# Attention, gated feed-forward and routed experts in one launch: load costs of the instruction planner, the low part of the weights, and softmax sums from a column of ones

## The chip, the cores and the metric

One core of one Trainium2 chip runs the kernel in a single launch. The metric is the device time of that launch in microseconds (us). The kernel before was run three times: 729.37, 726.54 and 720.55 us, median 726.54 us. One more execution was profiled; it took 723.54 us.

## The reference

Three layers follow each other.

- **Attention with hash buckets.** For 2 batches x 8 heads, 768 queries and 768 keys of 64 numbers. Six random projections give each query and key a bucket of 6 sign bits; a query sees only keys of its own bucket. `scores = q @ k.T / 8`, -1e9 where the buckets differ, then softmax over the keys and `attn @ v`. The softmax divides by `sum(exp) + 1e-9`.
- **A dense layer with a rational activation** on the 1536 x 512 result: `h = x @ w_in` (512 x 2048), `g = P(h) / Q(h)` with a cubic P and a quadratic Q, then `g @ w_out` (2048 x 512).
- **Routed experts.** Each of the 1536 rows goes to the expert of 8 with the largest logit: `relu(x @ w1[e]) @ w2[e]` (512 x 1024 x 512), scaled by its softmax weight and by a sigmoid gate.

All is float32. The kernel keeps the precision by splitting each operand into a high and a low float16 part, and sums three products (high x high, low x high, high x low).

## The kernel before, in words

**Stages.** 12 tiles of 128 rows. For each tile 8 heads are attended (96 in all), and each tile then passes the dense layer in 4 units (48 in all). The two run interleaved: the units of a tile begin some tiles behind its heads. When all tiles are through, the rows are ranked by expert, gathered in slots of 128 and sent through the experts (the last stage, from `early` and `final` to `tail`).

**A head** (`attend`, L518): TensorE makes the scores in PSUM (`scb`), VectorE takes their maximum (L533) and two small numbers (L534, L535), ScalarE takes the exponential into `p` and with `accum_out` its row sum into `den` (L540). A split (`split`, L284) makes a float16 high part on ScalarE or VectorE (L287) and a low part on GpSimd or VectorE (L288), both in `phl`. A transposing DMA turns them into `pT` (L544), and 18 matmuls with the split values VH and VL (L549 to L551) give 64 columns of PV in PSUM bank 0. The first `n32` = 7 heads go another way (`pv32`): transposed in float32 by TensorE, copied out of PSUM (L509), multiplied in float32 (L513). After each 4 heads `finish` (L553) forms the divisors `dn` from `den` (L561, L562), multiplies PV by them into `xf` (L563) and splits the result.

**The weights of the dense layer** come as 32 chunks of 512 KB (L402) in four buffers `tmp`. Each chunk holds its float32 numbers as halves of int64 words with scaled exponents; VectorE builds them with three integer instructions (L403, L404, L405). ScalarE then writes the high part WH, scaled by 256 (L406), scales the float32 chunk itself by 256 in place (L408), and GpSimd or VectorE subtracts (`WL = tmp - WH`, L409).

**What sets the order.** The program is written as a graph of operations, each with an engine (some with a choice of two), a cost, a DMA cost and a priority. `Graph.order` lays them out in time by these costs: it takes the operation that can start first, among those the one of the lowest priority number, and assigns a free operation to the engine that would end it first. Every engine's instructions then stand in the order of their planned starts, and each engine works them off strictly in that order on the chip. So a cost that is off does not change what is computed, but where an instruction stands: behind one that has to wait, it waits too. A load of 512 KB stands there with 1.456 us of the DMA queues. The table TUNE adds an offset to the priorities of each kind of operation (by its tag and by one of four parts of the program) and a bias to the choice of engine.

Of the kernel before, what the change touches and what calls it, by code (L numbers as in the profile page):

```python
# [25 lines left out]
TUNE = dict(lo=(0, 0, 1), w0=-6, n1=24, nb=[3, 3, 4, 4], nt=4, n2=4, q1=(1, 0), ck=[0, 1], ck2=[0, 0], cq=1, cq2=0, wq=1, wp=[1], wd=1.0, pq=3, pk=2, ld=5, lag=2.5, wdma=1.0, win=0.02, c0=0, cv=[2, 4], cv1=(0, 2), tc=4, ka=(0, 0, 0, 1), kb=(0, 0, 0, 0), wx=(0,), n32=7, vp=2, ev=(0, 0), c2=(1, 1, 1, 1), v2=(0, 0, 0, 0), fu=120, ff=14, fm=0.1, off={'cp': (-268.29, 167.43, -111.57, 0), 'ev': -227.13, 'ex': (660.02, 1353.36, 1191.8, 1674.11), 'f1': (-424.84, 428.14, -10.04, 621.04), 'f2': (-250.37, -7.79, -220.05, -301.11), 'f3': (-23.35, 4.25, 226.88, 33.9), 'f4': (-1229.72, -691.2, -403.07, -1036.86), 'f5': (208.7, 465.9, -29.69, 201.32), 'f7': (96.16, -302.05, -323.07, 73.51), 'f8': (-949.66, -1170.66, -563.08, -423.14), 'f9': (1185.88, 741.58, 588.87, 694.19), 'fa': (-813.71, -671.7, -732.04, -973.72), 'fb': (-76.95, -16.38, 5.69, 102.6), 'fi': (-682.61, -1081.59, -735.33, -615.52), 'gh': (-188.08, -241.89, -88.65, -81.64), 'gl': (475.63, 349.79, 802.09, 243.69), 'h': (-620.4, -273.02, -317.42, -644.08), 'hi': (749.27, 786.31, 760.64, 1215.18), 'k0h': 800.69, 'k0l': 127.42, 'kd': (-36.59, -32.48, 0, 0), 'kh': -286.24, 'kl': 26.57, 'lo': (471.66, -228.06, 668.92, 516.9), 'm2': (606.86, 1243.54, 1044.04, 1707.71), 'mx': (865.18, 876.13, 337.17, 72.6), 'pj': (332.41, -110.01, 246.4, 0), 'pv': (-157.74, -18.43, -210.46, -244.93), 'qh': (-522.1, -565.46, -401.0, 0), 'ql': (1130.36, 1000.63, 1003.49, 0), 'sc': (-674.28, -1622.43, -1312.02, -720.34), 'sg': (-1186.42, -501.8, -575.81, 0), 'tp': (-366.12, -394.82, 100.39, -477.05), 'tr': -356.17, 'v0h': 53.58, 'v0l': 122.21, 'v3': -200.82, 'vd': (103.76, 43.76, 0, 0), 'vh': -341.41, 'vl': -180.9, 'w1': 199.23, 'w2': 612.34, 'w3': 83.55, 'wd': -102.43, 'wh': 26.96, 'wl': 316.54, 'ws': 21.9, 'xd': (-547.65, 103.84, -621.18, -153.75), 'xh': (371.61, 427.76, 443.42, -215.44), 'xl': (-523.69, -754.73, -621.28, -525.38), 'xt': (-403.22, -1195.83, -1445.94, -248.18), 'xx': (159.21, -73.33, 571.84, -141.72), 'xy': (1693.3, 791.35, 722.59, 1567.91), 'xz': (443.87, -71.3, -641.46, -59.94)}, bias={'cp': (-7.42, 'ACT', 'ACT', 0), 'ev': 18.62, 'f3': (44.43, 25.58, 25.55, 39.82), 'gh': (0.32, 32.1, None, 22.27), 'gl': (30.91, 28.24, 3.36, 8.31), 'hi': (37.76, 60.01, 45.16, 50.31), 'k0h': -7.13, 'k0l': -29.55, 'kh': 'DVE', 'kl': -16.62, 'lo': (23.46, 27.97, 61.28, 7.14), 'qh': (7.28, -13.66, 25.19, 0), 'ql': (3.88, 12.77, 2.89, 0), 'v0h': 16.3, 'v0l': 17.12, 'vh': -3.05, 'vl': 13.82, 'wh': 11.09, 'wl': 0.49, 'ws': None, 'xh': None, 'xl': (0.16, 0.79, 'DVE', 2.33), 'xx': ('DVE', 'DVE', 'DVE', None)}, rel={('v', 0, 0): 28.6, ('v', 0, 1): 33.0, ('w', 3): 10.6, ('w', 1): 3.3, ('w', 4): 11.7, ('w', 2): 9.3, ('v', 0, 2): 0, ('v', 0, 3): 6.8})  # L26


class Graph:
# [19 lines left out]
    def op(self, eng, cost, fn, r=(), w=(), dma=0.0, prio=None, deps=(), tag=None, alt=(), rel=0.0):  # L49
# [243 lines left out]
def kernel_body(ctx, tc, qt_, kt_, v, proj, wio, ab, wg, w1, w2, cst, out):  # L293
# [811 lines left out]
```

## Time and profile before

| | before |
|---|---|
| median of 3 runs | 726.54 us (720.55 to 729.37) |
| profiled execution | 723.54 us |
| its span, first to last instruction | 721.8 us |
| mean granted TensorE clock | 0.969 |
| VectorE busy / ScalarE busy / GpSimd busy | 584.6 / 544.1 / 311.7 us |
| TensorE matmuls busy | 622.3 us |
| DMA, mean over the span | 165 GB/s |

How to read it: a busy time is a sum over stages with different limits. The last stage takes the span from about 522 us on. Matmuls are pipelined, each is recorded longer than the engine is held by it, so a busy TensorE is not one at its limit. In groups of instructions a line can be that of a helper (`split` has L287 and L288 for many tiles), so groups go by line and by tiles. The engines are named PE (TensorE), PEld (its weight loads), DVE (VectorE), ACT (ScalarE), POOL (GpSimd) and SP (the queue that issues the DMAs).

### The profile page before, as it was taken

The numbers are of one execution on the slowest core, as the hardware profiler recorded it, in microseconds if no ns is written. First come the engines' busy times: TensorE is split into PE (matmuls) and PEld (weight loads), VectorE is DVE, ScalarE is ACT, GpSimd is POOL, SyncE is SP. The second block draws the span as 40 slices with busy tenths as digits, with TensorE's granted clock in tenths as the row PEclk, the third lists the DMA queues.
The fourth block names the chain that finished last, engine by engine and source line by source line (L and its number), as shares of the span: only waits on it lengthen the run. The fifth ranks groups of instructions, "written<-read, shape, count | busy, mean of one in ns | idle before, by whom it ended". The sixth has DMA issues, their size and how long they took to land. (4 is left out here: it accounts for less than half of the span.)

```text
span 721.8 us, 19612 instructions
## 1 busy us (share of the span) xinstructions
PE 622.3 (86%) x7721; PEld 451.1 (62%) x7721; DVE 584.6 (81%) x1132; ACT 544.1 (75%) x885; POOL 311.7 (43%) x229
## 2 busy tenths in 40 slices
PE   0288699699998998989998999999689899989994
PEld 0146567567676765757776757777357577667762
DVE  5898778899998999795989996898949666576664
ACT  6587668889988888988996999987625565565663
POOL 2002326566656656476654574635403322122231
PEclk9999899799999999999999999999989999999997
DMA  8798639876969988979686496951753677799852
GB/s 273 232 221 275 177 93 209 173 117 120 169 104 174 190 150 182 173 137 183 127 158 132 83 164 122 169 91 24 208 144 88 126 205 248 251 243 264 230 132 40
DMA packets 230390, 119.04 MB, mean 165 GB/s; under 512 B 208398, under 2 KB 213390, under 8 KB 230288
## 3 DMA queue, kind: packets, MB, share of 16 engines
q1 hardware_dynamic: 227088, 111.37, 71.9%
q0 software_dynamic: 3200, 6.30, 2.6%
q8 instruction: 66, 1.08, 0.6%
q14 instruction: 36, 0.29, 0.1%
HBM read 83.15 MB, written 7.34 MB: 125 GB/s over the span
## 5 line engine op out<-in xcount | busy, mean ns | idle before, releaser
L288 POOL TENSOR_TENSOR phl<-p,phl 128x768 f16<-128x768 f32 x89 | 150.1, 1692 | 92.0 <-ACT phl L287 56.2
L598 PE MATMUL bank<-XT,WH 128*128 128x128 f16 x1440 | 130.4, 222 | 8.6 <-DVE tmp L620 5.4
L598 PEld LDWEIGHTS <-WH 128*128 128x128 f16 x1536 | 121.9, 99 | 20.5 <-issue 9.3
L932 DVE SCALAR_TENSOR_TENSOR WL<-st,WH 128x1024 f16<-128x1024 f32 x88 | 102.8, 1218 | 36.3 <-ACT WH L929 36.1
L598 PE MATMUL bank<-XT,WL 128*128 128x128 f16 x720 | 126.6, 221 | 0.0
L625 PE MATMUL bank<-WH,G 128*128 128x512 f16 x352 | 104.7, 379 | 4.8 <-DVE X L633 4.8
L540 ACT ACTIVATE p<-scb,sm 128x768 f32<-128x768 f32 x96 | 94.9, 990 | 14.1 <-DVE sm L535 6.9
L533 DVE TENSOR_REDUCE sm<-scb 128x1 f32<-128x768 f32 x96 | 90.4, 949 | 18.0 <-PE scb L527 12.9
L929 ACT ACTIVATE WH<-st 128x1024 f16<-128x1024 f32 x88 | 87.4, 1048 | 18.1 <-DMA st<-in_w 17.4
L625 PEld LDWEIGHTS <-G 128*128 128x128 f16 x576 | 52.2, 98 | 64.5 <-ACT G L287 3.5
L946 PEld LDWEIGHTS <-WH 128*128 128x128 f16 x1024 | 80.2, 99 | 9.9 <-issue 7.2
L288 POOL TENSOR_TENSOR G<-tmp,G 128x512 f16<-128x512 f32 x48 | 59.1, 1235 | 47.9 <-ACT G L287 44.9
L961 PE MATMUL bank<-WH,HT 128*128 128x512 f16 x256 | 76.7, 379 | 3.0 <-DVE HT L954 1.5
L969 POOL DMA_INDIRECT out<-OS,idx x16 | 21.8, 1361 | 131.5 <-ACT OS L965 101.2
L598 PEld LDWEIGHTS <-WL 128*128 128x128 f16 x768 | 76.1, 99 | 0.0
L287 ACT ACTIVATE phl<-p 128x768 f16<-128x768 f32 x89 | 74.2, 842 | 1.7 <-DMA pT<-phl 1.2
L625 PE MATMUL bank<-WL,G 128*128 128x512 f16 x176 | 66.7, 379 | 0.0
L946 PE MATMUL scb<-XGT,WH 128*128 128x128 f16 x704 | 62.2, 222 | 4.3 <-issue 2.4
L961 PEld LDWEIGHTS <-HT 128*128 128x128 f16 x384 | 36.6, 98 | 44.9 <-DVE HT L954 2.6
L946 PE MATMUL scb<-XGT,WL 128*128 128x128 f16 x352 | 61.3, 222 | 0.0
L527 PE MATMUL scb<-AK,AQ 128*128 128x384 f16 x192 | 47.8, 331 | 14.8 <-ACT p L540 14.7
L549 PE MATMUL bank<-VH,pT 128*128 128x64 f16 x534 | 53.8, 193 | 4.5 <-DMA pT<-phl 2.7
(229 smaller groups left out, 1568.3 us busy)
## 6 DMA issues: line engine op xcount, KB each, us to landing
st<-in_w SPq DMA_DIRECT2D x96, 512.0 KB
tmp<-in_wio SPq DMA_DIRECT2D x32, 512.0 KB
qraw<-in_qt_ SPq DMA_DIRECT2D x12, 256.0 KB
x2d<-X SPq DMA_DIRECT2D x12, 256.0 KB
kraw<-in_kt_ SPq DMA_DIRECT2D x5, 384.0 KB
vr<-in_v SPq DMA_DIRECT2D x5, 384.0 KB
AQ<-BQ SPq DMA_DIRECT2D x24, 64.0 KB
pT<-phl SPq DMA_TRANSPOSE x89
```

The lines of the kernel that those rows point to most:

```text
L287: g.op("ACT", c_act(n, 1), lambda: nc.scalar.activation(out=hi, in_=src, func=AF.Copy), r=rd, w=kh, prio=prio, tag=tags[0], alt=[("DVE", c ...
L288: f = lambda e: lambda: e.tensor_tensor(out=lo, in0=src, in1=hi, op=ALU.subtract)
L527: nc.tensor.matmul(sc[:, c], lhsT=A[0:k_, hh, p], rhs=K[0:k_, hh, c * 384:c * 384 + 384], start=st, stop=not st)
L533: g.op("DVE", 0.865, lambda: nc.vector.tensor_reduce(out=s[:, 0:1], in_=sc, axis=AX.XY, op=ALU.max), r=kb, w=[("mx", ks)], prio=prio, tag= ...
L540: g.op("ACT", 0.98, lambda: nc.scalar.activation(out=pf.rearrange("p (c n) -> p c n", c=2), in_=sc, func=AF.Exp, bias=s[:, 2:3], scale=s[: ...
L549: nc.tensor.matmul(o, lhsT=pt[:, k], rhs=VH[p][:, hh, k], start=(k == 0), stop=False)
L598: nc.tensor.matmul(hp[:, j * 128:j * 128 + 128], lhsT=w_[:, f, d * 128:d * 128 + 128], rhs=xt[:, hl * 4 + d], start=(k == 0), stop=(k == 11))
L625: nc.tensor.matmul(bank_f32(abank), lhsT=G_[:, gl, c0:c0 + 128], rhs=w_[:, f, 512:1024], start=(f == 0 and k == 0), stop=(f == FT - 1 and ...
L929: nc.scalar.activation(out=P["W"][k % 2][0][c], in_=P["st"][c], func=AF.Copy, scale=512.0)
L932: nc.vector.scalar_tensor_tensor(out=P["W"][k % 2][1][c], in0=P["st"][c], scalar=512.0, in1=P["W"][k % 2][0][c], op0=ALU.mult, op1=ALU.sub ...
L946: nc.tensor.matmul(o[:, (f % 4) * 128:(f % 4) * 128 + 128], lhsT=w_[f // 2][:, c0:c0 + 128], rhs=x_[:, hl * 4 + d], start=(n == 0), stop=( ...
L961: nc.tensor.matmul(bank_f32(6 + sub), lhsT=P["HT"][sub][:, hl, f], rhs=w_[4 + f // 2][:, c0:c0 + 512], start=(f == 0 and n == 0), stop=(f ...
```

## The change

1. **Load costs.** The planner's DMA cost of a 512 KB load goes from 1.456 to 1.95 us, of 384 KB from 1.092 to 1.45, of 256 KB from 0.728 to 0.97, and a load's data counts as landed 1.45 us after its queue time, no longer 0.97. A transposing DMA of `pT` goes from 1.9 to 2.0.
2. **Low part of the weights.** The scaling of `tmp` in place (L408) and the subtraction on GpSimd or VectorE are gone. One VectorE instruction per chunk makes `WL = tmp * 256 - WH`.
3. **Softmax sums.** VH gets a 65th column of ones, so the high x high and low x high matmuls give the sum of `p` in a 65th column of PV. The exponential loses its `accum_out` (except in the first 8 heads), and `finish` reads the sum from PSUM, after the matmuls.
4. `n32` goes from 7 to 8, and the table of offsets and biases is another one. Weight operations take their part of the table by chunk number.

```diff
-TUNE = dict(... wq=1, wp=[1], wd=1.0, ... n32=7, ... off={'cp': (-268.29, 167.43, -111.57, 0), ...
+TUNE = dict(... wq=1, wd=1.0, ... n32=8, ... off={'cp': (-4239.07, -2982.98, -3821.54, 0), ...
...
-                end = dma_free + 0.97
+                end = dma_free + (1.45 if cost == LD else 0.97)
...
-    VH, VL = ([tp(pa, f"{n}{i}", [128, 2, 6, D], F16) for i in range(HP)] for n in ("VH", "VL"))
+    VH, VL = ([tp(pa, f"{n}{i}", [128, 2, 6, d], F16) for i in range(HP)] for n, d in (("VH", D + 1), ("VL", D)))
...
-            if TUNE["wp"][k % len(TUNE["wp"])]:
-                g.op("ACT", c_act(512, 1), lambda tf=tf: nc.scalar.activation(out=tf, in_=tf, func=AF.Copy, scale=256.0), r=kt, w=kt, prio=pr, tag="ws", ...
-                g.op("POOL", c_pool(512), lambda ...: nc.gpsimd.tensor_tensor(out=WL[:, f, cl], in0=tf, in1=WH[:, f, cl], op=ALU.subtract), ..., tag="wl", alt=[("DVE", ...)])
-                continue
+            g.op("DVE", 0.6, lambda f=f, tf=tf, cl=cl: nc.vector.scalar_tensor_tensor(out=WL[:, f, cl], in0=tf, scalar=256.0, in1=WH[:, f, cl], op0=ALU.mult, op1=ALU.subtract), ..., tag="wl", part=k // 8)
...
+    pv3 = PV.rearrange("p (t d) -> p t d", d=D + 1)
+    for p in range(HP):
+        g.op("POOL", 0.1, lambda p=p: nc.gpsimd.memset(VH[p][:, :, :, D:D + 1], 1.0), w=[("V1", p)], prio=-28)
...
-        g.op("ACT", 0.98, lambda: nc.scalar.activation(out=pf.rearrange("p (c n) -> p c n", c=2), in_=sc, func=AF.Exp, bias=s[:, 2:3], scale=s[:, 1:2], accum_out=den[dk][:, h % 4:h % 4 + 1]), ...
+        ac = {"accum_out": den[dk][:, h % 4:h % 4 + 1]} if gi < N32 else {}
+        g.op("ACT", 0.975 if ac else 0.885, lambda: nc.scalar.activation(out=pf.rearrange("p (c n) -> p c n", c=2), in_=sc, func=AF.Exp, bias=s[:, 2:3], scale=s[:, 1:2], **ac), ...
...
-            o = PV[:, (h % 4) * 64:(h % 4) * 64 + 64]
+            o = pv3[:, h % 4]
             for k in range(6):
                 nc.tensor.matmul(o, lhsT=pt[:, k], rhs=VH[p][:, hh, k], start=(k == 0), stop=False)
-                nc.tensor.matmul(o, lhsT=pt[:, k], rhs=VL[p][:, hh, k], start=False, stop=False)
+                nc.tensor.matmul(o[:, 0:D], lhsT=pt[:, k], rhs=VL[p][:, hh, k], start=False, stop=False)
                 nc.tensor.matmul(o, lhsT=pt[:, 6 + k], rhs=VH[p][:, hh, k], start=False, stop=(k == 5))
...
-        d, e = dn[n % 2], den[n % 3]
+        d, e = dn[n % 2], den[n % 3] if 4 * n < N32 else pv3[:, :, D]
```

Where the change moves instructions is seen in the order of the rows on an engine. The first place is VectorE around the maximum of the very first head (`sm_123<-scb_70`; `tmp_143` to `tmp_146` are the four weight buffers, L403 to L405 the integer instructions). Before, from its 65th row on:

```order
L405 SCALAR_TENSOR_TENSOR tmp_144<-tmp_144 128x512
L403 TENSOR_SCALAR tmp_146<-tmp_146 128x512
L404 SCALAR_TENSOR_TENSOR tmp_145<-tmp_145 128x512
L404 SCALAR_TENSOR_TENSOR tmp_146<-tmp_146 128x512
L405 SCALAR_TENSOR_TENSOR tmp_145<-tmp_145 128x512
L405 SCALAR_TENSOR_TENSOR tmp_146<-tmp_146 128x512
L533 TENSOR_REDUCE sm_123<-scb_70 128x1
L533 TENSOR_REDUCE sm_124<-scb_71 128x1
```

And now, from the 113th row on (the new subtraction is L407, the maximum L532):

```order
L407 SCALAR_TENSOR_TENSOR WL<-tmp_143,WH 128x512
L405 SCALAR_TENSOR_TENSOR tmp_144<-tmp_144 128x512
L403 TENSOR_SCALAR tmp_145<-tmp_145 128x512
L404 SCALAR_TENSOR_TENSOR tmp_145<-tmp_145 128x512
L407 SCALAR_TENSOR_TENSOR WL<-tmp_144,WH 128x512
L405 SCALAR_TENSOR_TENSOR tmp_145<-tmp_145 128x512
L403 TENSOR_SCALAR tmp_146<-tmp_146 128x512
L404 SCALAR_TENSOR_TENSOR tmp_146<-tmp_146 128x512
L532 TENSOR_REDUCE sm_123<-scb_70 128x1
```

Before, 69 VectorE instructions stand ahead of the first maximum, among them 12 chunks built and 8 low parts; now 119, with 23 to 24 chunks built and 22 low parts. Up to the maximum of the 16th head the two come together again: 201 rows before (29 chunks begun, 24 low parts on VectorE), 210 now (30 and 29).

The second place is ScalarE at the first weight chunks, before:

```order
L406 ACTIVATE WH<-tmp_143 128x512
L406 ACTIVATE WH<-tmp_144 128x512
L408 ACTIVATE tmp_143<-tmp_143 128x512
L408 ACTIVATE tmp_144<-tmp_144 128x512
L406 ACTIVATE WH<-tmp_145 128x512
```

And now, with two copies of the first queries between the chunks:

```order
L406 ACTIVATE WH<-tmp_145 128x512
L406 ACTIVATE WH<-tmp_146 128x512
L446 ACTIVATE BQ_103<-BQ_103 64x512
L446 ACTIVATE AQ_101<-AQ_101 64x512
L406 ACTIVATE WH<-tmp_143 128x512
```

The 32 scalings are gone. Some operations with a choice of engine also change sides: over the whole program 9 of the 12 high parts X of the dense layer's result move from VectorE to ScalarE (L632), the high parts of 4 values V from VectorE to ScalarE, 8 of the 12 high parts BQ of the queries from ScalarE to VectorE, and 4 low parts `xn` from GpSimd to VectorE (L287, L288).

The third place is `finish` on VectorE in the middle of the program. Before, `dn_132` is formed from `den_130` right behind the `xf` of the group before it, and its own `xf` stands 26 rows further down:

```order
L563 TENSOR_TENSOR xf<-bank_66,dn_133 128x256
L561 TENSOR_SCALAR dn_132<-den_130 128x4
L615 SCALAR_TENSOR_TENSOR tmp_145<-tmp_145,co,bank_68 128x512
L562 RECIPROCAL dn_132<-dn_132 128x4
L534 TENSOR_SCALAR sm_125<-sm_125 128x1
```

And now (`bank_66` is PSUM bank 0 with PV):

```order
L561 TENSOR_SCALAR dn_132<-bank_66 128x4
L534 TENSOR_SCALAR sm_126<-sm_126 128x1
L562 RECIPROCAL dn_132<-dn_132 128x4
L615 SCALAR_TENSOR_TENSOR tmp_143<-tmp_143,co,bank_68 128x512
L563 TENSOR_TENSOR xf<-bank_66,dn_132 128x256
```

The divisors now stand right ahead of the `xf` that uses them, and wait for the same matmuls.

## Rows read from the trace of the kernel before

**Rows 1.** The page: busy us, share of the span, instructions of each engine.
```profile
PE   622.3 (86%) x7721; PEld 451.1 (62%) x7721; DVE 584.6 (81%) x1132; ACT 544.1 (75%) x885; POOL 311.7 (43%) x229
```

**Rows 2.** Busy us by stretch: PE, PEld, DVE, ACT, POOL; PEclk, DMA, GB/s.
```profile
0.00:44.00 44.00, 9.76 (x142) 6.49 (x143) 32.87 (x71) 26.22 (x39) 4.50 (x10) 1.00 0.86 252
44.00:121.00 77.00, 65.02 (x500) 45.24 (x498) 64.06 (x131) 58.16 (x108) 25.35 (x17) 0.91 0.73 189
121.00:522.00 401.00, 368.49 (x5083) 271.31 (x5080) 360.93 (x763) 349.47 (x605) 230.54 (x166) 0.98 0.78 143
522.00:722.00 200.00, 179.07 (x2002) 128.06 (x2002) 126.79 (x170) 110.28 (x134) 51.36 (x39) 0.96 0.67 180
```

**Rows 3.** Tile sm: the maxima, all 96; then VectorE at the 16th.
```profile
L533 DVE TENSOR_REDUCE sm<-scb x96: 925/948/959, 43.0 to 467.9; 128x1 f32<-128x768 f32 x96
...
120.17 0.96 DVE L533 TENSOR_REDUCE sm<-scb 128x1 f32<-128x768 f32 x1 [1.21 <-ACT p L540]
```

**Rows 4.** What VectorE waited for from 0 to 121 us: us, times, longest.
```profile
DVE tmp L403 <- DMA tmp<-in_wio: 11.3, 7, 4.1
DVE sm L533 <- PE scb L527: 6.6, 2, 5.7
```

**Rows 5.** The timeline around 80 us: start, us, engine, what, idle before.
```profile
80.41 5.46 POOL L288 TENSOR_TENSOR VL<-phl,VH 128x768 f16<-128x768 f32 x3 [3.66 <-ACT VH L287]
80.99 1.33 DVE L403 TENSOR_SCALAR tmp<-tmp 128x512 int32<-128x512 int32 x1 [2.34 <-DMA tmp<-in_wio]
82.25 2.12 DVE L404 SCALAR_TENSOR_TENSOR tmp<-tmp 128x512 int32<-128x512 int32 x1
84.30 2.12 DVE L409 TENSOR_TENSOR WL<-tmp,WH 128x512 f16<-128x512 f32 x1
...
86.80 2.82 PE L513 MATMUL bank<-phl,pT 128*128 128x64 f32 x12 [6.33 <-DVE xf L563]
```

**Rows 6.** Tile WL (ns least/median/most); groups by shape (busy us, mean ns, idle).
```profile
L932 DVE SCALAR_TENSOR_TENSOR WL<-st,WH x88: 1206/1217/1226, 515.7 to 711.3; 128x1024 f16<-128x1024 f32 x88
L409 DVE TENSOR_TENSOR WL<-tmp,WH x26: 678/684/2118, 20.9 to 131.6; 128x512 f16<-128x512 f32 x26
...
L409 POOL TENSOR_TENSOR WL<-tmp,WH 128x512 f16<-128x512 f32 x6 | 7.0, 1161 | 63.9 <-ACT tmp L408 63.9
L408 ACT ACTIVATE tmp<-tmp 128x512 f32<-128x512 f32 x32 | 19.2, 623 | 0.2
```

**Rows 7.** ScalarE's timeline at 88 us: two exponentials with their sums.
```profile
88.39 0.97 ACT L540 ACTIVATE p<-scb,sm 128x768 f32<-128x768 f32 x1
89.27 0.19 ACT L540 ACTIVATION_READ_ACCUMULATOR p<-scb,sm 128x1 f32 x1
89.36 0.97 ACT L540 ACTIVATE p<-scb,sm 128x768 f32<-128x768 f32 x1
```

**Rows 8.** Groups by shape, for dn by tile: operations that change sides; divisors; PV.
```profile
L632 DVE TENSOR_SCALAR X<-bank 128x512 f16<-128x512 f32 x9 | 6.1, 681 | 0.0
L632 ACT ACTIVATE X<-bank 128x512 f16<-128x512 f32 x2 | 1.2, 588 | 1.5 <-PE bank L625 1.5
L287 ACT ACTIVATE phl<-p 128x768 f16<-128x768 f32 x89 | 74.2, 842 | 1.7 <-DMA pT<-phl 1.2
L287 DVE CAST VH<-vr 128x768 f16<-128x768 f32 x4 | 3.0, 759 | 1.5 <-DMA vr<-in_v 0.8 <-PE bank L551 0.7
L287 ACT ACTIVATE BQ<-qraw 128x512 f16<-128x512 f32 x8 | 5.0, 627 | 0.2 <-PE scb L527 0.2
L287 DVE CAST BQ<-qraw 128x512 f16<-128x512 f32 x4 | 1.7, 432 | 1.8 <-PE scb L527 1.8
L288 DVE TENSOR_TENSOR xn<-xf,xn 128x256 f16<-128x256 f32 x12 | 5.4, 449 | 0.2 <-ACT xn L287 0.2
L561 DVE TENSOR_SCALAR dn<-den x24: 155/170/1517, 72.2 to 473.1; 128x4 f32<-128x4 f32 x24
L549 PE MATMUL bank<-VH,pT 128*128 128x64 f16 x534 | 53.8, 193 | 4.5 <-DMA pT<-phl 2.7 <-DVE OHK L431 1.0 <-DVE xf L563 0.5
```

More of the change, by code (lines that the diff above doesn't have):

```diff
@@ L72, in op @@
         prio = i if prio is None else prio
-        part = (prio >= 28) + (prio >= 60) + (prio >= 92)
+        part = (prio >= 28) + (prio >= 60) + (prio >= 92) if part is None else part
         self.raw.append((eng, cost, tuple(alt), tag, prio, part))
@@ L407, in kernel_body @@
-            if TUNE["wp"][k % len(TUNE["wp"])]:
-                g.op("ACT", c_act(512, 1), lambda tf=tf: nc.scalar.activation(out=tf, in_=tf, func=AF.Copy, scale=256.0), r=kt, w=kt, prio=pr, tag="ws", alt=[("DVE", c_dve(512, 2), lambda tf=tf: nc.vector.tensor_scalar(out=tf, in0=tf, scalar1=256.0, scalar2=None, op0=ALU.mult))])
-                g.op("POOL", c_pool(512), lambda f=f, tf=tf, cl=cl: nc.gpsimd.tensor_tensor(out=WL[:, f, cl], in0=tf, in1=WH[:, f, cl], op=ALU.subtract), r=kt + [("WH", f, c)], w=[("WL", f, c)], prio=pr, tag="wl", alt=[("DVE", c_dve(512), lambda f=f, tf=tf, cl=cl: nc.vector.tensor_tensor(out=WL[:, f, cl], in0=tf, in1=WH[:, f, cl], op=ALU.subtract))])
-                continue
@@ L411, in kernel_body @@
-            g.op("DVE", 0.6, lambda f=f, tf=tf, cl=cl: nc.vector.scalar_tensor_tensor(out=WL[:, f, cl], in0=tf, scalar=256.0, in1=WH[:, f, cl], op0=ALU.mult, op1=ALU.subtract), r=kt + [("WH", f, c)], w=[("WL", f, c)], prio=pr)
-    PV, BT, GT = bank_f32(0)[:, 0:256], bank_f32(0)[:, 384:456], bank_f32(0)[:, 480:496]
+            g.op(*wq, lambda f=f, ws=ws, cl=cl, we=we: we.dma_start(ws, wio[f, :, cl].bitcast(I32).rearrange("p (n t) -> p n t", t=2)), w=kw, dma=1.95, prio=pr, tag="wd", part=k // 8, rel=TUNE["rel"].get(("w", k), 0.0))
@@ new lines, in kernel_body @@
+            g.op("DVE", c_dve(512, 2), lambda hi_=hi_, t_=t_: nc.vector.tensor_scalar(out=t_, in0=hi_, scalar1=0x07FFFFFF, scalar2=3, op0=ALU.bitwise_and, op1=ALU.logical_shift_left), r=kw, w=kt, prio=pr, tag="w1", part=k // 8)
+            g.op("DVE", 0.6, lambda hi_=hi_, t_=t_: nc.vector.scalar_tensor_tensor(out=t_, in0=hi_, scalar=-(1 << 30), in1=t_, op0=ALU.bitwise_and, op1=ALU.bitwise_or), r=kw + kt, w=kt, prio=pr, tag="w2", part=k // 8)
+            g.op("DVE", 0.6, lambda lo_=lo_, t_=t_: nc.vector.scalar_tensor_tensor(out=t_, in0=lo_, scalar=29, in1=t_, op0=ALU.logical_shift_right, op1=ALU.bitwise_or), r=kw + kt, w=kt, prio=pr, tag="w3", part=k // 8)
@@ new lines, in kernel_body @@
+            g.op("ACT", c_act(512, 1), lambda f=f, tf=tf, cl=cl: nc.scalar.activation(out=WH[:, f, cl], in_=tf, func=AF.Copy, scale=256.0), r=kt, w=[("WH", f, c)], prio=pr, tag="wh", part=k // 8, alt=[("DVE", c_dve(512, 2), lambda f=f, tf=tf, cl=cl: nc.vector.tensor_scalar(out=WH[:, f, cl], in0=tf, scalar1=256.0, scalar2=None, op0=ALU.mult))])
+            g.op("DVE", 0.6, lambda f=f, tf=tf, cl=cl: nc.vector.scalar_tensor_tensor(out=WL[:, f, cl], in0=tf, scalar=256.0, in1=WH[:, f, cl], op0=ALU.mult, op1=ALU.subtract), r=kt + [("WH", f, c)], w=[("WL", f, c)], prio=pr, tag="wl", part=k // 8)
@@ L539, in attend @@
         pt, kpt = pT[gi % NPT], ("pT", gi % NPT)
-        g.op("ACT", 0.98, lambda: nc.scalar.activation(out=pf.rearrange("p (c n) -> p c n", c=2), in_=sc, func=AF.Exp, bias=s[:, 2:3], scale=s[:, 1:2], accum_out=den[dk][:, h % 4:h % 4 + 1]), r=kb + [("bi", ks), ("scl", ks)], w=[("p", ip), ("den", dk, h % 4)], prio=prio, tag="ex")
+        ac = {"accum_out": den[dk][:, h % 4:h % 4 + 1]} if gi < N32 else {}
+        g.op("ACT", 0.975 if ac else 0.885, lambda: nc.scalar.activation(out=pf.rearrange("p (c n) -> p c n", c=2), in_=sc, func=AF.Exp, bias=s[:, 2:3], scale=s[:, 1:2], **ac), r=kb + [("bi", ks), ("scl", ks)], w=[("p", ip)] + ([("den", dk, h % 4)] if ac else []), prio=prio, tag="ex")
         if gi < N32:
```

30 lines of the change are left out of this document (13 added, 17 removed).

## The prediction

> **What bounds the kernel now.** I read the page's busy times first, then the table by stretches, then VectorE's waits in the first stretch. The page [rows 1] names TensorE as the busiest engine, but its records overlap; VectorE with 584.6 us and ScalarE with 544.1 us are the engines that hold work one piece at a time. The stretches [rows 2] tell more. The reader is to see three things. From 121 to 522 us VectorE is busy 360.9 of 401 us, a share of 0.900, and ScalarE 349.5, a share of 0.871: both are near full and neither can be relieved alone. From 0 to 121 us VectorE is busy 32.9 + 64.1 = 96.9 us, so 24.1 us are idle, and this is the front in which the weights are loaded, at 252 GB/s for the first 44 us. From 522 us on the experts run with another balance, and the change issues nothing there.
>
> The front ends for me at the maximum of the 16th head, 120.17 us, which ends at 121.1 [rows 3]; the first maximum starts at 43.0. Of the idle 24.1 us, 11.3 are waits of the first weight instruction for its load, the longest 4.1 us at the start, and 6.6 are two waits of a maximum for scores [rows 4]. One place shows what a badly timed load does [rows 5]: the values V land when weights stand in VectorE's row, GpSimd makes three low parts VL in 5.46 us, and beside them three VectorE instructions take 1.33, 2.12 and 2.12 us. A 512-wide one of them takes 0.684 elsewhere [rows 6], so at least 5.57 - 2.05 = 3.5 us are stretch, and TensorE then stands 6.33 us for `xf`.
>
> A load of 512 KB at 252 GB/s takes 2.08 us. The planner had 1.456 and now has 1.95, so the rows it lays in the front should fit what happens.
>
> **The change part by part.** The sum is made against the profiled execution, 723.5 us.
>
> *Front.* The 32 low parts on VectorE are the same width as the 26 before, so I price them alike, 0.684 us [rows 6]. Up to the 16th maximum VectorE's row gets 5 low parts more (29 for 24: 3.4 us), 4 copies BQ at 0.432 (1.7) [rows 8], one chunk's three integer instructions (at most 2.0) and one pair of divisors less (0.3): +6.8 us. If the weights no longer stand beside the three VL, 3.5 us of stretch go. Work: 96.9 + 6.8 - 3.5 = 100.2 us. Idle: the first load remains, 4.1 us. Behind it the weights now come in an unbroken run, about 2 us of loading and 3 x 0.68 + less than 0.68 = 2.5 us of VectorE work per chunk at most, so VectorE should find them landed. I allow 6 us more: 10 in all. The front then ends at 110 us, a gain of 11. Bounds: with the idle time as before it ends at 124 (a loss of 3); with the first wait alone at 104 (a gain of 17). I take 10 us because the two causes that make 17.9 of the 24.1 us are those that the new row removes: the first maximum stands behind 50 instructions more, and its scores are long there.
>
> ScalarE in the front loses 28 scalings of 0.623 us [rows 6] and has slack to spare (84.4 of 121 us busy before [rows 2]).
>
> *From the 16th head to the last stage.* VectorE: 9 high parts X leave (9 x 0.681 = 6.1), 4 casts VH leave (4 x 0.759 = 3.0), 4 BQ come (1.7), 4 low parts `xn` come (4 x 0.449 = 1.8), one low part WL more (0.7), one chunk less (2.0) [rows 6, 8]. Sum -6.9: 354.0 us. At the share of 0.900 that takes 393.3 us, a gain of 7.7. ScalarE: an exponential with its sum starts at 88.39, its sum is read at 89.27 and the next starts at 89.36 [rows 7], so the reading holds the engine 0.09 us; 80 heads save 7.2. Further 4 scalings (2.5) and 4 BQ (2.5) go; 4 VH come at the 0.842 of the like copy (3.4), 9 X at 0.588 (5.3), one more high part (0.8) [rows 6, 8]. Sum -2.7: 346.8 us. In 393.3 us that is a share of 0.882 for ScalarE, more than the 0.871 it reached. So the saved ScalarE time is spent again on what VectorE gave away, and both engines would have to be fuller at once. I take half: 4 us. Bounds: 0, and 7.7.
>
> *Edits that I price at nothing.* The 65th column adds at most 1/64 to two of three PV matmuls, 0.8 us per 53.8 us of records [rows 8], on an engine that does not hold the end; if it did, 1.7 us. The divisors now read PSUM behind the matmuls and stand right ahead of `xf`: on VectorE the next maxima and activation rows wait behind them. The nearest row is the divisor on `den`, 0.155 us at least and 1.517 at most [rows 8]. If each of 22 waits lasted the whole difference, 30 us would be lost; if none is late, nothing, and the waits for `den` even go. The PV matmuls waited for `xf` 0.5 us in all [rows 8], so bank 0 was hardly ever held up at this place; I take 0, nearer to that row, and leave the upper end to the slow side of the range. The 8th float32 head swaps one high and one low part for two copies out of PSUM. The filler matmuls that fall away (75) are spare time of TensorE; the clock of 0.91 in 44 to 121 us [rows 2] could fall further, but VectorE's work does not follow TensorE's clock, and where the filler is missed the scores of two heads are late by microseconds, not the stage.
>
> Sum: 723.5 - 11 - 4 = 708.5 us. The profiled execution lies 3.0 us under the median of the runs, 726.5. I add these back and predict 711 us.
>
> *A rule against it.* The row: VectorE's L932, the same form of instruction with a float32 and a float16 operand from SBUF, takes 1.217 us for 1024 elements, and the subtraction L409 of the same two kinds 0.684 for 512 [rows 6]; twice the latter is 1.37, so the form costs nothing extra. The Trainium skill (Vector Engine (DVE) Microarchitecture Reference, section 7, Points that are easy to get wrong) says that such a scalar-tensor-tensor instruction with two SBUF sources that are not bf16 runs at half throughput. By that rule each of the 32 would take about the 1.217 of twice the width, 17 us more in the front, and the sum would be 728. The trace does not agree with it.
>
> **The rivals.**
>
> *Both engines fill up.* If the waits between VectorE and ScalarE shrink too, because the planner's costs fit, the later stage gains its 7.7 us and some 5 more and the front up to 17: 723.5 - 11 - 13 + 3 = 702, and with the front's 17 us 697. For it: 40.1 us of VectorE's 401 are idle [rows 2]. Against it: ScalarE would have to be busy at a share of 0.91.
>
> *The front's gain is given back.* The later stage is what it was: heads and dense units interleave at the pace of both engines, and a front that ends earlier meets the dense units no earlier. Then 723.5 +- 5, on the runs' scale 718 to 732. For it: the work of VectorE up to the 16th maximum is larger than before (+6.8), only idle time can pay. Against it: that idle time is 24.1 us, and two named waits make most of it.
>
> *Slower: the heads start late and keep their pace.* 50 VectorE instructions more stand ahead of the first maximum. At 0.684 us at most they are 34 us; of the 11.1 idle us in the first 44 [rows 2] some 7 are won back. So the first maximum comes at about 43 + 34 - 7 = 70 us. If the heads are then paced by their own chain of scores, exponential, transposes and matmuls, as later, (467.9 - 120.2) / 80 = 4.35 us each [rows 3], 15 heads take 65 us and the 16th maximum is at 135, 15 us late, and nothing behind makes it up: 723.5 + 15 + 3 = 741 us. It decides if the first 16 heads need more than 120 - 70 = 50 us. Against it: VectorE has only 100.2 - 66.9 = 33 us of work left between them, and ScalarE is lighter.
>
> *The halved instruction*, by the price above: 711 + 17 = 728 us.
>
> **How the numbers follow.** The forecast, 702 to 720 us with 711 the middle, gets 0.50; both engines filling up, 692 to 702, 0.12; the gain given back 0.25; the late heads 0.11; the halved instruction 0.02. Two per cent of 726.5 are 14.5 us, about what a measurement of this kernel tells from no change, so faster means under 712. Of the forecast's half a little over the lower half lies there, 0.31, and with the second case 0.43. Slower is the late heads and a tail of the divisors' waits, 0.12. The same keeps 0.45. The range goes from 694 to 732: it leaves out most of the late heads and the far end of the second case.
>
> **What would show it.** Right: the first maximum at 62 to 70 us and the 16th at 105 to 115; no wait of L403 over 4 us but the first; idle time of VectorE in the front near 10 us; no VL beside stretched weight instructions; L407 at 0.68 us. In the stretch from the 16th maximum to the experts, shares of VectorE and ScalarE of 0.90 and 0.87 or a little more, and no reading of accumulators but 8. Wrong: first to 16th maximum over 50 us; VectorE waiting for L549 to L551 at L561 in many groups; the 16th maximum early but the last stage begun no earlier than at 520 us; L407 near 1.2 us.

## The result and the profile after

The changed kernel takes 702.06 us in the median of 4 runs (701.16 to 703.58); the kernel before took 724.94 us in 4 runs (720.55 to 729.37). The ratio of the two is 0.9686 with a 95% interval of 0.9621 to 0.9752: faster by 3%. The profiled execution of the changed kernel took 703.58 us, with a span of 701.8. The ratios leave out executions that lie more than 1.5% above their kernel's fastest, at a lower granted TensorE clock: two of the four of e6 below, the profiled one among them, and one of the kernel before.

The page of the changed kernel, busy time by engine, beside [rows 1]:

```profile
PE 608.1 (87%) x7646; PEld 445.0 (63%) x7646; DVE 578.1 (82%) x1137; ACT 523.0 (75%) x771; POOL 298.1 (42%) x222
```

VectorE lost 6.5 us and ScalarE 21.1. That alone doesn't say where 20 us of span went; the stretches do. The table by stretch of the changed kernel, columns as in [rows 2], is cut where the 16th maximum ends (111.4 us) and where VectorE is through with the last of the 48 dense units (500.4; L620, which the expectations call the experts' last dense unit). The stretch up to the first cut is called the front below, the one between the cuts the middle.

```profile
0.00:111.40 111.40, 58.18 (x527) 41.56 (x528) 99.12 (x211) 67.82 (x108) 22.30 (x24) 1.00 0.79 227
111.40:500.40 389.00, 368.79 (x5101) 275.30 (x5100) 346.52 (x753) 342.47 (x526) 224.40 (x160) 0.98 0.80 148
```

And the kernel before, its middle stretch cut at the same two events (121.1 and 520.3):

```profile
121.10:520.30 399.20, 368.00 (x5080) 271.12 (x5077) 359.13 (x762) 348.53 (x604) 229.45 (x165) 0.98 0.78 143
```

The front shrank from 121.1 to 111.4 us (9.7), the middle from 399.2 to 389.0 (10.2), and what follows stayed: 721.8 - 520.3 = 201.5 before, 701.8 - 500.4 = 201.4 after. In the front VectorE has 99.1 us of work and 12.3 idle, where it had 97.0 and 24.1. In the middle its idle time didn't shrink (40.1 before, 42.5 after): the middle is shorter because VectorE has 12.6 us less work there, of which 2.4 went into more idle time.

The tile of the maxima, beside [rows 3]: the first starts at 67.9 us, and VectorE's timeline shows the 16th.

```profile
L532 DVE TENSOR_REDUCE sm<-scb x96: 926/948/958, 67.9 to 438.3; 128x1 f32<-128x768 f32 x96
```

```profile
110.41 0.94 DVE L532 TENSOR_REDUCE sm<-scb 128x1 f32<-128x768 f32 x1
```

What VectorE waited for from 0 to 121 us, beside [rows 4], the longest three:

```profile
DVE sm L532 <- PE scb L526: 3.2, 4, 1.9
DVE AK L287 <- DMA kraw<-in_kt_: 2.5, 1, 2.5
DVE WL L407 <- ACT WH L406: 2.1, 1, 2.1
```

No wait for a load of weights is among them, nor in the rest of that list; [rows 4] had 11.3 us of such waits. The new low part, beside L409 in [rows 6]:

```profile
L407 DVE SCALAR_TENSOR_TENSOR WL<-tmp,WH x32: 674/682/2133, 14.6 to 148.2; 128x512 f16<-128x512 f32 x32
```

The divisors, beside the `dn<-den` row of [rows 8]. There 24 of them took 11.0 us together (the group's sum in the profile), least 0.155 and most 1.517:

```profile
L562 DVE RECIPROCAL dn<-dn x24: 164/170/179, 79.5 to 457.5; 128x4 f32<-128x4 f32 x24
...
L561 DVE TENSOR_SCALAR dn<-bank x22: 148/154/163, 123.3 to 456.4; 128x4 f32<-128x4 f32 x22
```

From PSUM not one is over 0.163 us; all 24, with two from SBUF, take 3.7 us. What had stretched them is seen in the timeline of the kernel before at 379 us (start, us, engine, what):

```profile
379.22 1.64 POOL L288 TENSOR_TENSOR phl<-p,phl 128x768 f16<-128x768 f32 x1 [0.71 <-ACT phl L287]
379.37 1.52 DVE L561 TENSOR_SCALAR dn<-den 128x4 f32<-128x4 f32 x1
```

GpSimd's subtraction runs from 379.22 to 380.86; the divisor, four numbers a partition, starts at 379.37 and ends at 380.89, right behind it. In the kernel before 11 divisors began while a GpSimd instruction ran, and each of them ended 0.02 to 0.03 us after that instruction. After the change 11 of those that read PSUM began in the same way and none was stretched.

The divisors are not the only VectorE rows that became shorter. L613, which reads two whole tiles of SBUF, takes 38.3 us in its 48 instances where it took 42.2; its long ones, too, all began while GpSimd ran:

```profile
L613 DVE SCALAR_TENSOR_TENSOR tmp<-tmp,co 128x512 f32<-128x512 f32 x48 | 42.2, 884 | 6.0 <-ACT tmp L610 5.7
```

```profile
L613 DVE SCALAR_TENSOR_TENSOR tmp<-tmp,co 128x512 f32<-128x512 f32 x48 | 38.3, 801 | 8.5 <-ACT tmp L610 6.5 <-ACT tmp L611 1.8
```

### The profile page after: what moved, and what is told of

The parts are those of the page before. It is cut to its first block, busy times and chain, and to the rows that moved or that the text cites. A ratio compares the mean times of both kernels' runs of the same rounds, so it can differ in the third digit from the quotient of the medians.

```text
span 701.8 us, 19334 instructions
## 1 busy us (share of the span) xinstructions
PE 608.1 (87%) x7646; PEld 445.0 (63%) x7646; DVE 578.1 (82%) x1137; ACT 523.0 (75%) x771; POOL 298.1 (42%) x222
## 5 line engine op out<-in xcount | busy, mean ns | idle before, releaser
L288 POOL TENSOR_TENSOR phl<-p,phl 128x768 f16<-128x768 f32 x88 | 147.8, 1690 | 105.9 <-ACT phl L287 86.4
L932 DVE SCALAR_TENSOR_TENSOR WL<-st,WH 128x1024 f16<-128x1024 f32 x88 | 103.7, 1228 | 34.7 <-ACT WH L929 34.0
L532 DVE TENSOR_REDUCE sm<-scb 128x1 f32<-128x768 f32 x96 | 90.5, 949 | 16.7 <-PE scb L526 16.4
L287 ACT ACTIVATE phl<-p 128x768 f16<-128x768 f32 x88 | 73.3, 845 | 7.2 <-DMA pT<-phl 6.7
L288 POOL TENSOR_TENSOR G<-tmp,G 128x512 f16<-128x512 f32 x48 | 58.2, 1213 | 45.7 <-ACT G L287 31.9
L969 POOL DMA_INDIRECT out<-OS,idx x16 | 21.1, 1321 | 131.5 <-ACT OS L965 101.9
L946 PE MATMUL scb<-XGT,WH 128*128 128x128 f16 x704 | 60.6, 219 | 4.3 <-DVE X L633 3.2
L549 PE MATMUL bank<-VH,pT 128*128 128x65 f16 x528 | 56.1, 196 | 6.6 <-DMA pT<-phl 6.2
L946 PE MATMUL scb<-XGT,WL 128*128 128x128 f16 x352 | 59.7, 219 | 0.0
L549 PEld LDWEIGHTS <-pT 128*128 128x128 f16 x528 | 49.3, 97 | 13.8 <-DMA pT<-phl 10.0
```

Source lines behind the costliest of these rows:

```text
L287: g.op("ACT", c_act(n, 1), lambda: nc.scalar.activation(out=hi, in_=src, func=AF.Copy), r=rd, w=kh, prio=prio, tag=tags[0], alt=[("DVE", c ...
L288: f = lambda e: lambda: e.tensor_tensor(out=lo, in0=src, in1=hi, op=ALU.subtract)
L532: g.op("DVE", 0.865, lambda: nc.vector.tensor_reduce(out=s[:, 0:1], in_=sc, axis=AX.XY, op=ALU.max), r=kb, w=[("mx", ks)], prio=prio, tag= ...
L549: nc.tensor.matmul(o, lhsT=pt[:, k], rhs=VH[p][:, hh, k], start=(k == 0), stop=False)
L932: nc.vector.scalar_tensor_tensor(out=P["W"][k % 2][1][c], in0=P["st"][c], scalar=512.0, in1=P["W"][k % 2][0][c], op0=ALU.mult, op1=ALU.sub ...
L946: nc.tensor.matmul(o[:, (f % 4) * 128:(f % 4) * 128 + 128], lhsT=w_[f // 2][:, c0:c0 + 128], rhs=x_[:, hl * 4 + d], start=(n == 0), stop=( ...
```

## The experiments

Two theories stood after the result. A: the middle's gain is the divisors, which no longer wait for GpSimd, and the accumulator readings matter little. B: it is the accumulator readings, or the moved work between the two engines, as the prediction had it. For the front: the loads' costs, the table of places, or the scalings. The kernel before, run on the same chip as each set of four experiments, took 728.08 us (e1 to e4), 726.39 (e5 to e8) and 722.64 (e9 to e12), so ratios are compared rather than times.

**Sums in SBUF again, in the new order (e1).** All exponentials hand out sums, and the divisor reads them where it now stands.

```diff
-ac = {"accum_out": den[dk][:, h % 4:h % 4 + 1]} if gi < N32 else {}
+ax = {"accum_out": den[dk][:, h % 4:h % 4 + 1]}
-d, e = dn[n % 2], den[n % 3] if 4 * n < N32 else pv3[:, :, D]
+d, e = dn[n % 2], den[n % 3]
```

> The changed kernel with every row in its place; the sums come again from the exponential (accum_out in all 96 heads) and the divisors are formed from den in SBUF, at their new place ahead of xf. The matmuls still make the 65th column, which nobody reads. Theory A (the later stage got shorter because VectorE no longer stands in the divisors, and ScalarE no longer reads accumulators): the 22 divisors take 0.3 to 0.5 us again instead of 0.154, 4 to 7 us of VectorE, and ScalarE is held 0.09 us more in 88 heads, 8 us; the time rises by 5 to 12 us, to 707 to 714. Theory B (the new order alone does it): 700 to 704.

717.44 us, ratio 0.9841 (0.9808 to 0.9874), more than the 714 that theory A allowed. Its middle, and its divisors:

```profile
111.40:511.00 399.60, 371.49 (x5101) 275.59 (x5100) 357.80 (x754) 350.30 (x607) 223.41 (x160) 0.98 0.76 144
```

```profile
L562 DVE TENSOR_SCALAR dn<-den x24: 154/192/1598, 79.1 to 467.3; 128x4 f32<-128x4 f32 x24
```

The middle takes 399.6 us, as long as in the kernel before (399.2): with the sums in SBUF nothing of the middle's gain is left. The 24 divisors take 13.5 us together, 2.5 more than in the kernel before. The last stage, in which no instruction was changed, takes 205.6 us instead of 201.4 (204.0 in e2 below); why stays open.

**The sums handed out, but not read (e2).** Only the first of the two edits above.

> As the changed kernel in every row, but the exponential also writes its sum in all 96 heads, and nobody reads it (the divisors still come from PSUM). Only ScalarE's 0.09 us in 88 heads come back, 8 us of an engine that is busy at a share of 0.88 in the later stage. Theory A: at that share most of it is paid, 4 to 8 us, 706 to 710. Theory B: ScalarE waits often enough to hide it, 701 to 704. The difference to the kernel with den is what the divisors alone cost: 3 to 6 us if GpSimd holds them up, 0 otherwise.

708.29 us, ratio 0.9725 (0.9695 to 0.9755), the middle:

```profile
112.10:502.30 390.20, 368.02 (x5102) 273.74 (x5101) 348.90 (x754) 348.54 (x607) 223.33 (x160) 0.99 0.80 147
```

ScalarE carries all accumulator readings again, 6.1 us more work in the middle than in the changed kernel, and the middle is 1.2 us longer. Between e2 and e1 only the divisor's operand differs, and the middle grows by 9.4 us, VectorE's work by 8.9, the divisors by 9.8 (13.5 against 3.8). So in the new order reading the sums from PSUM is worth 9.4 us of the middle and not handing them out 1.2. That the two together come near the middle's 10.2 is in part chance: e1's divisors were held longer than those of the kernel before, which had at most 11.0 - 3.7 = 7.3 us to give back.

**One more small instruction from SBUF (e9).** The converse, with the divisors left in PSUM:

```diff
 nc.vector.reciprocal(out=d[:, 4:8], in_=d[:, 0:4])
+if 4 * n >= N32:
+    nc.vector.tensor_scalar(out=den[n % 3], in0=d[:, 0:4], scalar1=1e-9, scalar2=2.0**-8, op0=ALU.add, op1=ALU.mult)
```

> The changed kernel with one more VectorE instruction right behind each of the last 22 reciprocals: the same 128x4 add-and-multiply as the divisor's, from SBUF to SBUF, its result not read. The divisors still read PSUM. Theory A, GpSimd holds such an instruction until its own subtraction is over: the 22 extra ones take 8 to 13 us together where their own work is 22 x 0.16 = 3.5 us, the stretch from the 16th maximum to the experts' last dense unit grows by 6 to 12 us against the changed kernel's 389.0, and the time is 707 to 714 us at 725 before. Rival, the hold-up belonged to the accumulator's hand-over in e1: the extra ones take 3.5 to 4.5 us and the time grows by 2 to 4 us, 704 to 706.

710.47 us, ratio 0.9829 (0.979 to 0.9868). The extra instruction, and the middle:

```profile
L565 DVE TENSOR_SCALAR den<-dn x22: 137/728/1622, 124.1 to 464.3; 128x4 f32<-128x4 f32 x22
```

```profile
111.30:507.10 395.80, 368.64 (x5101) 274.59 (x5100) 357.60 (x775) 343.57 (x526) 224.99 (x160) 0.99 0.79 145
```

The same operation on the same shape takes 0.154 us in the median from PSUM and 0.728 from SBUF. The 22 take 16.6 us, more than expected, and the middle grows by 6.8. All 14 that began while GpSimd ran were held until 0.02 to 0.03 us after its end; the other 8 took 0.140 us at most. No accumulator is in play here, so theory A stands: the hold-up by GpSimd is shown, and that it costs time in this stretch.

**Sums handed out to PSUM (e5).**

```diff
+ax = ac or {"accum_out": bank_f32(0)[:, 260 + 4 * dk + h % 4:261 + 4 * dk + h % 4]}
-d, e = dn[n % 2], den[n % 3] if 4 * n < N32 else pv3[:, :, D]
+d, e = dn[n % 2], den[n % 3] if 4 * n < N32 else bank_f32(0)[:, 260 + 4 * (n % 3):264 + 4 * (n % 3)]
```

> The changed kernel's order; from the third group of heads on the exponentials hand their sums to 12 unused fp32 places of PSUM bank 0 instead of SBUF, and the divisor reads them there; the column of ones is still multiplied and its sums are not read. Everything else is as in the run that keeps the sums in SBUF (e1). Theory A, GpSimd holds up a VectorE instruction whose operands both lie in SBUF: the 24 divisors take 3.7 to 4.5 us together instead of 13.5, the stretch from the 16th maximum to the experts' last dense unit takes 389 to 392 us instead of 399.6, and the kernel 703 to 709 us at 725 before. Rival, it is the accumulator's late hand-over or the divisor's place in the order: the divisors keep 10 us or more and the time stays with that of e1, 712 to 718.

738.05 us, ratio 1.0166 (1.0103 to 1.023): a miss of both. The divisors and TensorE's longest wait in the middle:

```profile
L562 DVE TENSOR_SCALAR dn<-bank x22: 147/161/163, 128.4 to 491.6; 128x4 f32<-128x4 f32 x22
```

```profile
PE bank L550 <- ACT p L541: 16.2, 15, 2.1
```

The divisors behave as theory A says, never over 0.163 us. But the exponentials now write into bank 0, where TensorE sums the values' products and the projections stand, and the products wait for the exponentials, 16.2 us, a wait that e1 doesn't show. The time of this run says nothing of the divisors; whether the shared bank alone makes the wait stays open.

**The scaling put back on ScalarE, in the new order (e3).**

```diff
 nc.scalar.activation(out=WH[:, f, cl], in_=tf, func=AF.Copy, scale=256.0)
+nc.scalar.activation(out=tf, in_=tf, func=AF.Copy, scale=256.0)
-nc.vector.scalar_tensor_tensor(out=WL[:, f, cl], in0=tf, scalar=256.0, in1=WH[:, f, cl], op0=ALU.mult, op1=ALU.subtract)
+nc.vector.tensor_tensor(out=WL[:, f, cl], in0=tf, in1=WH[:, f, cl], op=ALU.subtract)
```

> The changed kernel with every row in its place; each of the 32 weight chunks is again scaled in place by ScalarE right behind its high part, and the low part is a plain subtraction on VectorE. ScalarE gets 32 x 0.62 us back, 24 to 28 of them in the front, where it is busy 68 of 111 us. My forecast priced the scalings' loss at nothing: then 701 to 705, the subtraction waiting for the scaling a few times. Rival (the scaling stood between high and low part and so in VectorE's chain of weights): each low part waits some 0.3 to 0.5 us longer for ScalarE, the front grows by 7 to 15 us, 709 to 717.

713.65 us, ratio 0.9787 (0.9754 to 0.9821). VectorE's longest wait in the front:

```profile
DVE WL L410 <- ACT tmp L408: 8.7, 12, 2.6
```

The 16th maximum comes at 118.1 us, 6.7 late, and the middle is nearly unchanged (388.4 us). In the front the low parts come one chunk after the other, and 12 times VectorE now waits for one more ScalarE instruction behind the high part. The one fused instruction is worth nearly 7 us there, in this order, and as a shorter chain: ScalarE, put back to 85 us of work, is still idle for 33 of the 118.

**The new instructions in the old order (e4).** The kernel before, its order unchanged, with the fused low part, the column of ones and the divisors from PSUM (divisor and reciprocal stand right ahead of the normalization); the scalings issue nothing.

```diff
-nc.gpsimd.tensor_tensor(out=WL[:, f, cl], in0=tf, in1=WH[:, f, cl], op=ALU.subtract)
+nc.vector.scalar_tensor_tensor(out=WL[:, f, cl], in0=tf, scalar=256.0, in1=WH[:, f, cl], op0=ALU.mult, op1=ALU.subtract)
...
-d, e = dn[n % 2], den[n % 3]
+d, e = dn[n % 2], den[n % 3] if n < 2 else pv3[:, :, D]
```

> The kernel before with its own order of rows and its own table, but with the instructions of the change: no scaling, the low part of all 32 chunks by one VectorE instruction at the old place, the 65th column, no sums by the exponential behind the 8th head, and divisors from PSUM, right ahead of xf. If the instructions bring the gain in any order (theory A): the later stage gains 7 to 12 us, the front 0 to 4, 710 to 718. If the order brings it (theory B): 721 to 728. In between, both are needed.

734.45 us, ratio 1.0086 (1.0052 to 1.012), slower than either theory allowed. VectorE's longest waits from 0 to 531 us:

```profile
DVE sm L540 <- PE scb L534: 24.1, 20, 5.2
DVE tmp L403 <- DMA tmp<-in_wio: 11.6, 8, 4.2
```

The waits for weights are those of the kernel before (11.3 there), and the maxima wait for scores, 24.1 us where the kernel before has 12.9. The divisors are short (3.75 us), yet the middle takes 408.4 us. The instructions bring nothing in an order that wasn't laid for them; how much of the loss is the divisor's new place in VectorE's chain stays open.

**Load costs and table apart (e6, e8).** Both have the changed instructions and are laid anew: e6 with the load costs of before, e8 with the table of before.

```diff
-dma=1.95
+dma=1.456
-end = dma_free + (1.45 if cost == LD else 0.97)
+end = dma_free + 0.97
```

> The changed kernel, its order laid anew with the load costs of the kernel before (1.456, 1.092, 0.728, transposes 1.9, landing 0.97 after), table and instructions as changed. Theory A, the loads' costs bring the front's gain: VectorE and ScalarE wait for loads again in the first 121 us (5 us or more more of waits for a DMA than the changed kernel's), the 16th maximum ends at 118 to 124 us, and the kernel takes 709 to 717 us at 725 before. Rival B, the table of places brings it and the loads come out early enough either way: 16th maximum at 110 to 114, kernel 700 to 706. A third way: any new laying of the order loses, since the table was found for one set of costs; then the control with a load cost of 1.94 (e7) loses as much as this one.

> The changed kernel with the new load costs and instructions, but with the table of places (offsets and engines' biases) of the kernel before. Theory A, load costs and instructions bring the front's gain, the table little: 16th maximum by 116 us, kernel 700 to 712. Rival B, the table's order (all weights first, heads late) brings it: first maximum near 44 us again, 16th at 119 to 125, kernel 712 to 735.

e6: 756.25 us, ratio 1.0334 (1.0231 to 1.0437). e8: 760.99, ratio 1.0462 (1.0386 to 1.0538). The maxima of e6, then of e8:

```profile
L532 DVE TENSOR_REDUCE sm<-scb x96: 929/950/959, 48.1 to 472.9; 128x1 f32<-128x768 f32 x96
```

```profile
L532 DVE TENSOR_REDUCE sm<-scb x96: 929/950/959, 70.4 to 472.9; 128x1 f32<-128x768 f32 x96
```

Both lose more than any theory gave. One thing is plain: the load costs, not the table, put the weights ahead of the heads. With the new costs the first maximum starts at 67.9 (changed kernel) and 70.4 us (e8), with the old ones at 43.0 [rows 3] and 48.1 (e6). The 16th ends at 117.9 us in e6 and at 119.3 in e8. What VectorE waited for loads of weights up to 121 us, e6, then e8:

```profile
DVE tmp L403 <- DMA tmp<-in_wio: 1.7, 3, 0.9
```

```profile
DVE tmp L403 <- DMA tmp<-in_wio: 4.0, 1, 4.0
```

With old costs and the old table these waits were 11.3 us, in e4 11.6. Either the new costs or the new table thus takes most of them away, so the load costs are not the one cause that theory A made them. Yet neither front ends near 111 us. How the front's gain divides between the two these runs can't say, as the controls show.

**Controls: one load cost moved by less than one per cent (e7, e11, e12).** 1.94 and 1.96 for 1.95 in the changed kernel, 1.466 for 1.456 in the kernel before.

> The control for e6: the changed kernel, its order laid anew with 1.94 for 1.95 as the cost of a load of weights, which moves no landing by more than some tenths of a us. If the table's order is not tied to the exact costs: 700 to 706 us, 16th maximum at 110 to 114. If every new laying loses: 708 us or more, and e6 tells nothing of the loads.

> A second control on the order: the changed kernel laid anew with 1.96 for 1.95 as the cost of a load of weights. If the table fits only the one set of costs, as the run with 1.94 suggests: 715 to 740 us, with the front's end (16th maximum) within 2 us of 111 and the loss in the stretch behind it. If 1.94 was bad luck: 700 to 706.

> The same control on the kernel before: its order laid anew with 1.466 for 1.456 as the cost of a load of weights. If its table fits its one set of costs in the same way: 738 to 760 us at 725 before, as much lost as in the changed kernel, so that the two kernels compare like with like. If it stays at 722 to 730, the changed kernel alone owes part of its gain to a luckier fit.

722.63 us (ratio 0.9947, 0.9911 to 0.9984), 735.95 (1.0185, 1.0136 to 1.0233) and 746.41 (1.0326, 1.0258 to 1.0393). The middles of e7, e11 and e12:

```profile
111.00:511.60 400.60, 367.06 (x5086) 274.25 (x5084) 344.80 (x736) 339.17 (x523) 223.22 (x158) 0.99 0.76 135
```

```profile
111.80:529.30 417.50, 378.69 (x5106) 279.40 (x5104) 355.88 (x748) 344.54 (x526) 222.47 (x158) 0.96 0.76 135
```

```profile
115.30:541.50 426.20, 381.05 (x5083) 278.83 (x5081) 350.67 (x753) 346.57 (x598) 222.50 (x159) 0.95 0.74 129
```

The front of the changed kernel stands firm, 111.0 and 111.8 us; that of the kernel before moved from 121.1 to 115.3, so more than half of the front's 9.7 us lies within what a new laying does to it. The middles don't hold: VectorE's share falls from 0.891 to 0.861 and 0.852, in the kernel before from 0.900 to 0.823. In e11 ScalarE waits more for VectorE, above all here (1.9 us in the changed kernel):

```profile
ACT G L287 <- DVE tmp L620: 15.3, 12, 2.9
```

In these three tries each table fits the one set of costs that it was made for. Against the fitted order, a new laying costs 0.026 and 0.050 of the time in the changed kernel and 0.033 in the kernel before, 19 to 36 us at 725. The two kernels as measured are both at their fitted order; e6 and e8 are not, and no single cost can be read off their times. A rival stays: part of the 3% can be that the new table fits better than the old one did. With both kernels off their fitted order the changed one is still ahead, 0.9947 and 1.0185 against 1.0326, by 3.7 and 1.4%, but three such orders are too few to give the share.

**The reciprocal from PSUM itself (e10).** Here one VectorE instruction a group is left out.

```diff
-nc.vector.reciprocal(out=d[:, 4:8], in_=d[:, 0:4])
+nc.vector.reciprocal(out=d[:, 4:8], in_=e if late else d[:, 0:4])
-nc.vector.tensor_tensor(out=xf, in0=pv3[:, :, 0:D], in1=dd, op=ALU.mult)
+nc.vector.scalar_tensor_tensor(out=xf, in0=pv3[:, :, 0:D], scalar=256.0, in1=dd, op0=ALU.mult, op1=ALU.mult)
```

> The changed kernel without the last 22 divisor instructions: the reciprocal reads the sums in PSUM itself, and the scaling by 256 goes into the normalization, which takes two multiplications in one instruction; the 1e-9 added to the sums is left out there. If VectorE is what the stretch waits for: 22 x (0.103 occupied) = 2.3 us go, 700 us at 725 before, a ratio 0.003 below the changed kernel's. Rival, the chain of the order absorbs it: no difference, 701 to 703. If the two multiplications cost more than one (0.422 us in the trace of after): slower by up to 22 x 0.3 = 6 us.

704.56 us, ratio 0.9746 (0.9708 to 0.9784), beside 0.9686 for the changed kernel, whose interval overlaps it: no gain shown. The middle is 0.6 us shorter (388.4) for 1.5 us less VectorE work, and the last stage longer by as much and more (203.1 us). No version that beats the changed kernel came out of these runs.

## Why the prediction was right, and where its terms were off

Forecast 711 us, measured 702.06, inside the range and at the lower end of the forecast's own case; faster by 3%, the side that had 0.43. On the profiled executions the sum was 708.5 and the time 703.58, so 4.9 us are terms of the sum; the rest is the 3.0 us that were added back because the profile of before lay under its median, while that of after lies 1.5 over.

*Front: right in size, in part by luck.* Forecast a gain of 11 and the 16th maximum at 110; measured 9.7 and 111.4. Work 100.2 forecast, 99.1 measured; idle time 10 forecast, 12.3 measured. The two causes named went: the waits for loads of weights, even the first one of 4.1 us that the forecast kept, and half of the wait for scores (6.6 to 3.2). Weight instructions are still stretched beside VL, one of 2.14 us at 80 us and one of 1.68 at 90, so less than half of the 3.5 us for that was won, and that sign of being right failed.

*Scalings: priced at nothing, wrongly reasoned.* "ScalarE in the front loses 28 scalings ... and has slack to spare" looked at ScalarE's sum. In the new order the scaling would stand between the high and the low part in VectorE's own chain, and e3 shows that it costs 6.7 us there. With the scalings back the front ends at 118.1 us, a gain of 3.0: 6.7 of the 9.7 us hang on an edit that the forecast gave no gain. Its idle time of 10 us counted no wait for ScalarE between the parts of a chunk, and so the total came out.

*Middle: mechanism half seen, size off.* The step that failed is "So the saved ScalarE time is spent again ... and both engines would have to be fuller at once. I take half: 4 us", and under it the sum of VectorE's work, -6.9. Measured: a gain of 10.2 with 12.6 us less VectorE work. Two things were wrong.

First, the divisors were priced at 0 as a possible wait, though [rows 8] had them at 0.155 to 1.517 us. That spread was the very thing that the change removes: GpSimd's subtractions held them. Between the two kernels it is 7.3 us of VectorE's work (6.4 in the middle); put back into the new order (e2 to e1) it costs 9.4. The rest of the 12.6 us is not taken apart by a run. The work counted as moved did move, 6.1 us of X and 3.0 of VH, but brought less than the 6.9 us counted: e1 has all of it, and its VectorE work in the middle is 357.8 us beside 359.1, some 4 us less if its longer divisors (2.5) are set aside. The same hold-up took some of it back and gave some elsewhere: the low parts `xn` on VectorE take 0.65 us each in the middle after (14 of them, 9.1 us), where each was reckoned at 0.449, and L613 lost about 4.

Second, the halving. Within the new order the middle followed VectorE's work: its share is 0.895 in e1, 0.894 in e2, 0.891 after, 0.903 in e9, 0.888 in e10. ScalarE went to 0.880 after and to 0.893 in e2, above the 0.871 at which the prediction saw it full. So in this order VectorE bound the stretch, and ScalarE was no second ceiling at these shares. That the middle's gain would come from VectorE's work was right; the rows that give most of it, and the half that was taken off, were not. The waits for `den` went, as forecast (in the middle the divisors waited 4.5 us for ScalarE before, 1.6 for TensorE after), but other waits took their place.

The Trainium skill (SBUF — State Buffer, section Who interferes with whom) says that VectorE and GpSimd share a pair of SBUF ports, which the one that issues first gets for the whole instruction while the other blocks; on VectorE's side it concerns instructions in a two-port mode, which tensor-scalar ones can enter, and those with two SBUF inputs, these against a GpSimd instruction that reads SBUF. The trace agrees: 11 of 11 divisors before and 14 of 14 extra ones in e9 were held, and none of the 11 with its operand in PSUM. In which mode the divisors ran no run shows. Read against the diff, that rule could have named the term that was left out.

*The rivals.* "Both engines fill up" gave 702, the measured time, but not by its mechanism: it let the waits between VectorE and ScalarE shrink and the later stage gain 13 us, while VectorE's idle time in the middle rose (40.1 to 42.5 us) and the gain was 10.2. That its number was hit is luck. "The gain is given back" fell with the middle. "The heads start late" came true in its first half, with the first maximum at 67.9 us (70 forecast), but from there to the 16th maximum it took 43.5 us, under the 50 at which it decided. The halved instruction is refuted: L407 takes 0.682 us beside 0.684 for the plain subtraction of the same two kinds. The rule that the prediction cites for it, in the Vector Engine (DVE) Microarchitecture Reference of the Trainium skill, section 7 (Points that are easy to get wrong), shows no effect on these two operands.

*The order.* That an order may be worth more than the instructions in it was in no case of the prediction. The controls show 19 to 36 us from the order alone, about the whole measured gain or more.

## What to carry to other kernels

A row whose longest instance is ten times its shortest may hide a wait: look up whether GpSimd ran each time that it was long, and whether an operand can come from PSUM instead. Before relief on a second engine is counted or discounted, ask whether its instruction stands in the first engine's chain; busy sums don't show that. And where a planner's table was fitted to exact costs, compare fitted with fitted and test a part of the change by instructions that leave the order alone: a new laying cost 19 to 36 us here, more than the 3 to 11 us of the parts tested in e1, e2, e3 and e9.

## What the runs showed of the hardware

Held up behind GpSimd's subtractions were the 128x4 additions from SBUF (in e9 to 1.622 us, 0.137 at least) and instructions with two whole operands in SBUF, as L613, whose longest was 1.41 us in the changed kernel and 0.745 in the median. A held 128x4 one ended 0.02 to 0.03 us after GpSimd's; the five held `xn` of the changed kernel (128x256, 0.419 us in the median) ended 0.28 after it, and the two held L407 (128x512, 0.682) 0.55 after it, so most of their own work lay behind the wait. The reciprocal of the same 128x4 tile, SBUF to SBUF, never passed 0.179 us in the changed kernel, though 13 of the 24 began while GpSimd ran; and the two 128x1 instructions on `sm` (L533, L534) never passed 0.217 us there. VectorE's low parts of the last stage (L932) run beside GpSimd's indirect DMAs without being held: 39 of the 88 did in the changed kernel, none over 1.23 us. The one that met a GpSimd subtraction, at 502 us, took 2.18.
